# Attention with mixed heads and two MoE layers: value products leave PSUM one step later, between the reciprocals and the post-mix

## Chip, cores and metric

One NeuronCore of one Trainium2 chip runs the whole program. The metric is the device time of one execution in microseconds (us), as the median of several runs. Engines are named as in the profile: PE (TensorE matmul), PEld (TensorE weight load), DVE (VectorE), ACT (ScalarE), POOL (GpSimd), SP (SyncE, which issues DMAs).

## What is computed

Two batches, 12 heads, 448 positions, head size 64. The scores of all heads are mixed by a 12x12 matrix ahead of the softmax, and the attention weights by another one behind it. The result, 896 rows of 768, goes through two feed-forward layers. Cut from the reference:

```
scores = scale * np.matmul(q, k.transpose(0, 1, 3, 2))
scores = np.einsum('bhij,hg->bgij', scores, w_pre)
scores = scores - np.max(scores, axis=-1, keepdims=True)
attn = np.exp(scores)
attn = attn / (np.sum(attn, axis=-1, keepdims=True) + 1e-09)
attn = np.einsum('bhij,hg->bgij', attn, w_post)
x = np.matmul(attn, v)            # then laid out as 896 x 768
h = x @ w_in;  g = h * np.clip(h + 3.0, 0.0, 6.0) / 6.0;  x = g @ w_out
h = x @ w_in2; g = np.maximum(h, 0.0) + alpha * np.minimum(h, 0.0); out = g @ w_out2
```

## The kernel before

The query rows are cut into 8 tiles of 120, 120, 120 and 88 rows for each batch. Each tile is cut into groups of 10 rows (120 rows of the mixing: 10 rows times 12 heads), 90 groups in all. A main loop takes two groups (a pair) in each of its steps; step p, from 0 to 44, works on pair p. The order of the instructions on every engine is the order in which this loop is written, there is no scheduler behind it. In the middle of the loop a step issues:

- PE: the pre-mix of pair p (tile name mx, L199), then one scores product of a later tile (sc, L174), then the post-mix of pair p-1 (pt, L238), then a value product (av, L281), most often one, at some steps two, at some none.
- DVE: two maxima over mx (nm, L205), half of the copies of sc into S (L551), the reciprocals of the sums (sm, L221 and L222). ACT: two exponentials (e, L214), the other half of the copies of S, two copies of pt into MT (L253). POOL scales the post-mix weights by the reciprocals (wr, L226); in the last 8 steps DVE does it. Both also convert weights of the first feed-forward layer in some steps (wb, wst, whi, wlo).

`av(ti, a)` makes the value product of heads 2a and 2a+1 of tile ti: 16 instructions, which the trace shows as 32 passes. They go into two PSUM tiles, `av_ps[0][0]` for one half of the keys (z = 0) and `av_ps[0][1]` for the other (z = 1); the order within the product alternates between the two. Three values of a fill the pair of tiles. The pool has `bufs=2` for the tag "av", so there is just this one pair of them: when a is 0 or 3, the next three products need both tiles empty again.

A full pair is emptied ("evacuated") by one ACT copy of the first tile into xT (L291) and one DVE addition of the second tile to it (L292); 88-row tiles take two of each. Before the change both stand right behind the third product, at the end of that step.

The eight PSUM banks are all in use: two each for mx, pt, av and sc.

The places of the value products, step by step, follow from `av_at`: the third and the sixth product of a tile (a = 2 and a = 5) fall into steps 9, 12, 15, 18, 20, 22, 25, 28, 31, 34, 37, 40, 43 and 44 for tiles 0 to 6. The first product of the next three falls into the very next step at 10, 13, 16, 19, 21, 26, 32 and 38. Behind steps 22, 28, 34 and 40 there is a step without a value product first (23, 29, 35, 41). In step 43 the next product stands in the same step.

Of the kernel before, what the change touches and what calls it, by code (L numbers as in the profile page):

```python
# [7 lines left out]
F32 = mybir.dt.float32  # L8
# [5 lines left out]
ALU = mybir.AluOpType  # L14
# [21 lines left out]
def kernel(  # L36
# [15 lines left out]
    nc = tc.nc  # L52
    _, D, H, S = k.shape
# [14 lines left out]
    tiles = []  # L68
    groups = []
    for b in range(B):  # L70
        for i0 in range(0, S, GP):
            n = min(GP, S - i0)
# [8 lines left out]
    NTILE, NG = len(tiles), len(groups)  # L81
# [25 lines left out]
    with tc.manual_schedule():  # L107
        xT = xtp.tile([128, KD, NT], F32, name="xT")
# [23 lines left out]
        def load_q(ti, *at, qs=(nc.sync, nc.sync)):  # L132
            T = tiles[ti]
            n = T["n"]
            m = H // 2 * n
            t = q_st[ti] = kq.tile([128, Z + H // 2 * GP], F32, tag="qst", bufs=2, name="qst")
            nc.gpsimd.memset(t[:, :Z], 0.0)
            z = Q + m - n + upper(n)
            if z > Z + m:
                nc.gpsimd.memset(t[:, Z + m:z], 0.0)  # L140
            at = (0, *at, H // 2)
            for x, y in zip(at, at[1:]):
                for o in range(2):
                    d = slice(D * o, D * o + D)
                    a = T["i0"] * H
                    src = q[T["b"], d, a:a + H * n].rearrange("p (j o n) -> p j o n", o=2, n=n)
                    qs[o].dma_start(
                        out=t[d, Z + x * n:Z + y * n].rearrange("p (j n) -> p j n", n=n),
                        in_=src[:, x:y, o, :],
                    )  # L150
                yield
# [33 lines left out]
        def pull(g, q=nc.sync):  # L185
            ti, o, st, xn = groups[g]
            d = d_buf[g // 2 % len(d_buf)]
            src = S_t[ti][bass.ds(Z + o, xn, step=st)] if st > 1 else S_t[ti][Z + o:Z + o + xn]
            q.dma_start(d[Z:Z + xn * H, g % 2, :], src)
# [19 lines left out]
        def exp(p):  # L209
            ms, nms = mx_t.pop(p)  # L210
            sm = sm_t[p] = late.tile([128, 2], F32, tag="sm", bufs=2, name="sm")
            for o in range(2):
                e = late.tile([128, S], F32, tag="e", bufs=4, name="e")
                nc.scalar.activation(  # L214
                    out=e, in_=ms[o][:, :S], func=ACTF.Exp, bias=nms[o], accum_out=sm[:, o:o + 1]
                )
                e_t[2 * p + o] = e

        def norm(p):
            sm = sm_t.pop(p)  # L220
            nc.vector.tensor_scalar(sm, sm, 1e-9, None, ALU.add)  # L221
            nc.vector.reciprocal(sm, sm)  # L222
            for o in range(2):
                wr = wr_t[2 * p + o] = late.tile([128, WP], F32, tag="wr", bufs=4, name="wr")
                eng = nc.gpsimd if p < late_from else nc.vector
                eng.tensor_scalar(wr, wpost, sm[:, o:o + 1], 1.0, ALU.mult, ALU.mult)  # L226
# [32 lines left out]
        def by_row(dst, src, n):  # L259
            m = n // G * G  # L260
            d, s = dst[..., :m], src[..., :m]
            if len(dst.shape) == 3:
                yield (d.rearrange("p z (x o) -> p z x o", x=G), s.rearrange("p z (o x) -> p z x o", x=G))
            else:
                yield (d.rearrange("p (x o) -> p x o", x=G), s.rearrange("p (o x) -> p x o", x=G))
            if n > m:
                yield dst[..., m:n], src[..., m:n]

        av_ps = {}

        def av(ti, a):
            T = tiles[ti]
            n = T["n"]
            if a % 3 == 0:
                av_ps[0] = [psA.tile([128, 3, GP], F32, tag="av", bufs=2, name="av") for _ in range(2)]
            p = av_ps[0]
            for t in range(NJ):
                for o in range(2):
                    for z in range(2):
                        h = 2 * a + o  # L280
                        nc.tensor.matmul(  # L281
                            p[z][64 * o:64 * o + 64, a % 3, :n],
                            v_t[T["b"], h // HC][Q * z:Q * z + JH, h % HC, t, :],
                            MT[ti][Q * z:Q * z + JH, t, h, :n], start=(t == 0), stop=(t == NJ - 1),
                            skip_group_check=True,
                        )
            if a % 3 == 2:
                c0 = T["b"] * S + T["i0"]
                x = xT[:, a - 2:a + 1, c0:c0 + n]
                for (d, s0), (_, s1) in zip(by_row(x, p[0][:, :, :n], n), by_row(x, p[1][:, :, :n], n)):  # L290
                    nc.scalar.copy(d, s0)  # L291
                    nc.vector.tensor_tensor(d, s1, d, ALU.add)  # L292
                if ti >= NTILE - 2:
                    b0 = T["i0"]
                    h, l = (y[:, a - 2:a + 1, b0:b0 + n] for y in x_pairs(1))
                    nc.scalar.copy(h, x)
                    nc.vector.tensor_tensor(l, x, h.bitcast(F32), ALU.subtract)

        qk_at, av_at = {}, {}
        for i in range((NTILE - 1) * (H // 2)):  # L300
# [118 lines left out]
        def ptile():  # L419
            if "ps6" not in P:  # L420
                return P["ps2"].tile([128, 512], F32, tag="p", name="p")
            n_ps[0] += 1
            where = P["ps6"] if n_ps[0] % 8 < 6 else P["ps2"]
            return where.tile([128, 512], F32, tag="p", name="p")
# [4 lines left out]
        def x_all(c):  # L429
            return [P[f"x{c}"].tile([128, KD, S], R, tag=f"x{z}", name=f"x{z}") for z in "hl"]  # L430

        def x_pairs(c):
            if (0, c) not in x_t:
                xs = x_all(c)
                for kk in range(KD):
                    x_t[kk, c] = [x[:, kk, :] for x in xs]
                x_whole[c] = xs
            return x_whole[c]
# [16 lines left out]
        def in_part(p, i, xs, c, k0, k1):  # L455
            for kk in range(k0, k1):
                mm3(p, [w[:, kk, :] for w in w_t[i]], xs[kk, c], kk == 0, kk == KD - 1)

        def in_chain(i, xs, c):
            p = ptile()[:, :S]  # L460
            in_part(p, i, xs, c, 0, KD)
            return p
# [32 lines left out]
        def run(a):  # L495
            for _ in a:
                pass
# [33 lines left out]
        for c in range(2):  # L531
            a = GH * c
# [3 lines left out]
        for c in range(2):  # L536
            a = GH * c
# [24 lines left out]
        for i in range(NC):  # L562
            a = 2 * (14 + 8 * i)
# [35 lines left out]
        for p_ in range(-2, NP + 1):  # L599
            if p_ == -2:  # L600
                for g in range(6):
                    if g == 2:
                        list(load_q(2))
                    pull(g)
            late_pull = None
            if 0 <= p_ < NP - 3:
                g = 2 * p_ + 6
                pull(g)
                if groups[g][0] == groups[g + 1][0]:
                    pull(g + 1)  # L610
                else:
                    late_pull = g + 1
            for f in load_at.get(p_, []):
                f()
            for ti in load_q_at.get(p_, []):
                list(load_q(ti))
            if 0 <= p_ < NP:
                premix(p_)
            two = [lambda ti=ti, j=j: qk(ti, j, "mx" if p_ < 0 and j % 2 else "sc") for ti, j in qk_at.get(p_, [])]
            pend = [f() for f in (two if p_ < 0 else two[:1])]  # L620
            if 0 <= p_ < NP:
                exp(p_)
            for s_ in pend:
                s_out(s_)
            if p_ >= 0:
                for f in two[1:]:
                    s_out(f())
            if late_pull:
                pull(late_pull)
            if 0 <= p_ < NP:  # L630
                norm(p_)
            if 1 <= p_:
                post(p_ - 1)
                post_evac(p_ - 1)
            kk = 2 * (p_ - (NP - KD // 2))
            if kk == 0:
                p0 = ptile()[:, :S]
            if 0 <= kk < KD:
                in_part(p0, 0, x_t, 0, kk, kk + 2)
            if p_ == NP:  # L640
                p1 = in_chain(1, x_t, 0)
                gs[0, 0] = g_tile(0, 0)
                run(act1(p0, gs[0, 0], 0))
            for f in also.get(2 * p_, []) + also.get(2 * p_ + 1, []):
                f()
            for ti, a in av_at.get(p_, []):
                av(ti, a)
# [2 lines left out]
                f()  # L650
        for a in range(H // 2):
            av(NTILE - 1, a)
        p2 = in_chain(2, x_t, 0)
        gs[1, 0] = g_tile(1, 0)
        run(act1(p1, gs[1, 0], 1))
# [6 lines left out]
        for f in range(NC):  # L662
            p = in_chain(f, x_t, 1)
# [134 lines left out]
```

## Time and profile before

| | |
|---|---|
| median of 3 runs | 663.63 us (663.16 to 666.03) |
| the profiled execution, its own time | 661.99 us |
| its span, first to last instruction | 660.2 us |
| PE busy | 636.3 us (96%) |
| DVE, ACT, POOL busy | 408.2, 353.2, 291.3 us (62%, 53%, 44%) |
| value products (av), first to last start | 40.3 to 202.2 us |

The profile gives times in us from the start of the span. A row of the order of time reads: start, duration, engine, line, operation, tile written <- tiles read, shapes, count, and in brackets how long the engine sat idle before it and what ended this wait. Nearly the whole span is PE's; the attention part, with the steps of the loop, lies in front of 203 us, and the feed-forward layers fill the rest.

### The profile page before, as it was taken

The page shows a single profiled execution, that of the slowest core. Times are in us where ns is not written, and L with a number is a line of the kernel's source. Part 1 is how long each engine was busy: PE and PEld are TensorE (multiplying, and loading weights), DVE is VectorE, ACT ScalarE, POOL GpSimd, SP SyncE. Part 2 cuts the span into 40 slices and gives each one's busy share as a digit, 9 for nine tenths or more (in the row PEclk, how much of TensorE's full clock was granted, in tenths as well). Part 3 has the DMA queues.
Part 4 walks back from the last instruction along what each step waited for, and adds up shares of the span by engine and source line. Part 5 has one row for each costly group of instructions (what it writes and reads, how often), then busy time and mean ns, then how long its engine had stood idle before and what let it go on. Part 6 is the DMA issues. An engine that isn't in the chain of part 4 may idle for free.

```text
span 660.2 us, 17587 instructions
## 1 busy us (share of the span) xinstructions
PE 636.3 (96%) x7464; PEld 558.9 (85%) x7464; DVE 408.2 (62%) x640; ACT 353.2 (53%) x664; POOL 291.3 (44%) x236
## 2 busy tenths in 40 slices
PE   7996999998899999999999999999999999999997
PEld 2575776686688999999999999999999999999997
DVE  4664565756446678888543643389999998334501
ACT  4785787787774665666443443434444444443310
POOL 2121131312633445545675554445554556776430
PEclk9999999999899999999999999999999999999999
DMA  6776654654401233233343233212332223445202
GB/s 167 234 241 172 181 158 150 209 182 112 145 3 49 96 129 111 97 105 133 98 144 143 96 103 137 96 50 96 109 124 102 96 95 120 139 144 208 97 0 84
DMA packets 34923, 81.82 MB, mean 124 GB/s; under 512 B 11420, under 2 KB 24988, under 8 KB 34844
## 3 DMA queue, kind: packets, MB, share of 16 engines
q1 hardware_dynamic: 34268, 80.27, 37.3%
q8 instruction: 59, 0.97, 0.6%
q10 hardware_dynamic: 576, 0.41, 0.2%
q14 instruction: 20, 0.16, 0.1%
HBM read 58.65 MB, written 2.75 MB: 93 GB/s over the span
## 4 chain that ended last, share of the span: by engine, by line
PE 78%; ACT 6%; issue 5%; POOL 4%; DMA 3%; DVE 3%; SPq 0%; POOLq 0%; ACTq 0%; DVEq 0%
PE p L451 62%; PE pt L238 5%; PE mx L199 5%; PE av L281 4%; PE sc L174 3%; ACT e L214 3%; POOL wb L373 2%; POOL wlo L384 2%; ACT MT L253 1%; DMA kst<-in_k_dram 1%; DVE nm L205 1%; DVE xT L292 1%; DMA qst<-in_q_dram 1%; DMA pull<-S 1%; ACT S L551 1%
## 5 line engine op out<-in xcount | busy, mean ns | idle before, releaser
L384 POOL TENSOR_TENSOR wlo<-wb,whi 128x768 fp32r<-128x768 f32 x64 | 126.1, 1971 | 140.2 <-ACT whi L378 140.2
L373 POOL TENSOR_TENSOR wb<-wb,wst 128x768 int32<-128x768 int32 x64 | 125.6, 1963 | 74.5 <-DVE wb L366 64.9
L451 PE MATMUL p<-xh,whi 128*128 128x448 f32 x384 | 140.2, 365 | 0.0
L451 PE MATMUL p<-xl,whi 128*128 128x448 f32 x384 | 139.7, 364 | 0.0
L451 PE MATMUL p<-gl,whi 128*128 128x448 f32 x384 | 139.4, 363 | 0.0
L451 PE MATMUL p<-gh,whi 128*128 128x448 f32 x384 | 139.2, 362 | 0.0
L451 PE MATMUL p<-xh,wlo 128*128 128x448 f32 x384 | 138.5, 361 | 0.0
L451 PE MATMUL p<-gh,wlo 128*128 128x448 f32 x384 | 138.4, 360 | 0.1
L358 DVE TENSOR_SCALAR wb<-wb 128x768 f32<-128x768 f32 x64 | 52.0, 812 | 82.8 <-ACT wb L342 82.8
L342 ACT ACTIVATE wb<-wst 128x768 f32<-128x768 f32 x64 | 58.0, 907 | 70.2 <-DMA wst<-in_w_out_dram 52.2
L378 ACT CAST whi<-wb 128x768 fp32r<-128x768 f32 x64 | 53.3, 833 | 50.4 <-PE p L451 32.3
L238 PEld LDWEIGHTS pt<-wr,e 60*64 60x64 f32 (+1 forms) x2880 | 59.8, 135 | 22.1 <-issue 11.4
L214 ACT ACTIVATE e<-mx,nm 128x448 f32<-128x448 f32 x90 | 56.4, 634 | 39.8 <-DVE nm L205 39.7
L451 PEld LDWEIGHTS p<-xh,whi 128*128 128x128 f32 x384 | 72.3, 188 | 6.1
L451 PEld LDWEIGHTS p<-gh,whi 128*128 128x128 f32 x384 | 72.1, 188 | 5.7
L451 PEld LDWEIGHTS p<-gh,wlo 128*128 128x128 f32 x384 | 71.8, 187 | 5.5 <-POOL wlo L384 0.5
L451 PEld LDWEIGHTS p<-xh,wlo 128*128 128x128 f32 x384 | 72.0, 188 | 5.2
L226 POOL TENSOR_SCALAR wr<-wpost,sm 128x60 f32<-128x60 f32 x74 | 25.3, 356 | 115.4 <-DVE sm L222 112.8
L451 PEld LDWEIGHTS p<-xl,whi 128*128 128x128 f32 x384 | 72.4, 188 | 3.6
L451 PEld LDWEIGHTS p<-gl,whi 128*128 128x128 f32 x384 | 72.1, 188 | 3.7
L366 DVE SCALAR_TENSOR_TENSOR wb<-wst,wb 128x768 uint32<-128x768 uint32 x64 | 67.5, 1055 | 1.1
L238 PE MATMUL pt<-wr,e 60*64 60x60 f32 (+1 forms) x2880 | 60.7, 221 | 7.1 <-issue 6.1
(50 smaller groups left out, 792.4 us busy)
## 6 DMA issues: line engine op xcount, KB each, us to landing
wst<-in_w_out_dram SPq DMA_DIRECT2D x32, 768.0 KB
wst<-in_w_in_dram SPq DMA_DIRECT2D x27, 768.0 KB
pull<-S SPq DMA_DIRECT2D x88, 210.0 KB
wst<-in_w_in_dram SPq DMA_DIRECT2D x10, 384.0 KB
v<-in_v_dram SPq DMA_DIRECT2D x16, 168.0 KB
out_dram<-o SPq DMA_DIRECT2D x12, 224.0 KB
qst<-in_q_dram SPq DMA_DIRECT2D x8, 180.0 KB
kst<-in_k_dram SPq DMA_DIRECT2D x4, 336.0 KB
```

Of the source, the lines that this page charges most:

```text
L199: nc.tensor.matmul(ms[r][Q * c:Q * c + Q, :S], wpre[a:z], d[a:z, c, :], start=True, stop=True)
L214: nc.scalar.activation(out=e, in_=ms[o][:, :S], func=ACTF.Exp, bias=nms[o], accum_out=sm[:, o:o + 1])
L226: eng.tensor_scalar(wr, wpost, sm[:, o:o + 1], 1.0, ALU.mult, ALU.mult)
L238: nc.tensor.matmul(ts[c][Q * z:Q * z + m, u:u + GH], e[a:a + GH, j:j + m], wr[a:a + GH], start=True, stop=True,)
L281: nc.tensor.matmul(p[z][64 * o:64 * o + 64, a % 3, :n], v_t[T["b"], h // HC][Q * z:Q * z + JH, h % HC, t, :], MT[ti][Q * z:Q * z + JH, t, ...
L342: nc.scalar.activation(t, s[:, :, 1].bitcast(F32), ACTF.Abs)
L358: nc.vector.tensor_scalar(t, t, W_MAX, W_MIN, ALU.min, ALU.max)
L366: nc.vector.scalar_tensor_tensor(u, st_t[i][:, :, 1], 0xC0000000, u, ALU.bitwise_and, ALU.bitwise_or)
L373: nc.gpsimd.tensor_tensor(n, n, st_t.pop(i)[:, :, 0].bitcast(I32), ALU.add)
L378: nc.scalar.copy(hi, b_t[i])
L384: nc.gpsimd.tensor_tensor(lo, b_t.pop(i), w_t[i][0].bitcast(F32), ALU.subtract)
L451: nc.tensor.matmul(p, wt[a], xt[c], start=(first and z == 0), stop=(last and z == 2))
```

## The change

The evacuation moves into a function of its own, `av_evac`. When the third product of a group is issued, the pair of tiles is only noted in a list. The list is emptied at one of three places, whichever comes first: at the next product with a = 0 or 3 (ahead of taking the tiles again), in the next step behind `norm(p_)` (reciprocals and scaled weights) and in front of `post(p_ - 1)`, or at the end of the attention part. No instruction is added or removed.

```
+        def av_evac():
+            while full:
+                ti, a, p = full.pop()
...
+                for (d, s0), (_, s1) in zip(by_row(x, p[0][:, :, :n], n), by_row(x, p[1][:, :, :n], n)):
+                    nc.scalar.copy(d, s0)
+                    nc.vector.tensor_tensor(d, s1, d, ALU.add)
...
         def av(ti, a):
             T = tiles[ti]
             n = T["n"]
             if a % 3 == 0:
+                av_evac()
                 av_ps[0] = [psA.tile([128, 3, GP], F32, tag="av", bufs=2, name="av") for _ in range(2)]
...
             if a % 3 == 2:
-                c0 = T["b"] * S + T["i0"]
-                x = xT[:, a - 2:a + 1, c0:c0 + n]
-                for (d, s0), (_, s1) in zip(by_row(x, p[0][:, :, :n], n), by_row(x, p[1][:, :, :n], n)):
-                    nc.scalar.copy(d, s0)
-                    nc.vector.tensor_tensor(d, s1, d, ALU.add)
...
+                full.append((ti, a, p))
...
             if 0 <= p_ < NP:
                 norm(p_)
+            av_evac()
             if 1 <= p_:
                 post(p_ - 1)
                 post_evac(p_ - 1)
...
         for a in range(H // 2):
             av(NTILE - 1, a)
+        av_evac()
```

ACT around the first evacuation (it belongs to the products of steps 7 to 9), before; a pair of exponentials begins each step:

```order
L214 ACTIVATE e,sm<-mx,nm 128x448 x2
L551 COPY S<-sc 92x448
L253 COPY MT<-pt 120x48x10 x2
L291 COPY xT<-av 128x3x120
L214 ACTIVATE e,sm<-mx,nm 128x448 x2
L551 COPY S<-sc 92x448
L253 COPY MT<-pt 120x48x10 x2
```

and after:

```order
L214 ACTIVATE e,sm<-mx,nm 128x448 x2
L559 COPY S<-sc 92x448
L253 COPY MT<-pt 120x48x10 x2
L214 ACTIVATE e,sm<-mx,nm 128x448 x2
L559 COPY S<-sc 92x448
L279 COPY xT<-av 128x3x120
L253 COPY MT<-pt 120x48x10 x2
```

The copy out of av now stands behind the two exponentials and the copy of S of step 10 and ahead of that step's two copies out of pt.

DVE at the same place, before; a pair of maxima begins each step:

```order
L205 TENSOR_REDUCE nm<-mx 128x1 x2
L551 COPY S<-sc 92x448
L221 TENSOR_SCALAR sm<-sm 128x2
L222 RECIPROCAL sm<-sm 128x2
L292 TENSOR_TENSOR xT<-av,xT 128x3x120
L205 TENSOR_REDUCE nm<-mx 128x1 x2
L551 COPY S<-sc 92x448
L221 TENSOR_SCALAR sm<-sm 128x2
L222 RECIPROCAL sm<-sm 128x2
```

and after:

```order
L205 TENSOR_REDUCE nm<-mx 128x1 x2
L559 COPY S<-sc 92x448
L221 TENSOR_SCALAR sm<-sm 128x2
L222 RECIPROCAL sm<-sm 128x2
L205 TENSOR_REDUCE nm<-mx 128x1 x2
L559 COPY S<-sc 92x448
L221 TENSOR_SCALAR sm<-sm 128x2
L222 RECIPROCAL sm<-sm 128x2
L280 TENSOR_TENSOR xT<-av,xT 128x3x120
```

The addition stood ahead of the maxima of step 10 and now stands behind its reciprocals. The order on PE, POOL and SP is the same as before. On PE step 10 ends so, after the change; the last three rows are the first value product of the next three:

```order
L238 MATMUL pt<-wr,e 64x60 [waits Activation_49,Pool_49]
L238 MATMUL pt<-wr,e 64x60 [waits Activation_49]
L238 MATMUL pt<-wr,e 64x60 x12
L238 MATMUL pt<-wr,e 56x60 x2
L238 MATMUL pt<-wr,e 64x60 [waits Pool_49]
L238 MATMUL pt<-wr,e 64x60 x13
L238 MATMUL pt<-wr,e 56x60 x2
L298 MATMUL av<-MT,v_692 64x120 [waits DMAHW1_49,PE_49,Activation_49]
L298 MATMUL av<-MT,v_692 64x120 [waits DMAHW2_49,DVE_49,PE_49]
L298 MATMUL av<-MT,v_692 64x120 x14
```

The first instruction of the product waits for ACT and the second for DVE, that is for the copy and for the addition of the group before.

The same move is made at 12 places: the evacuations that ran at the start of steps 10, 13, 16, 19, 21, 23, 26, 29, 32, 35, 38 and 41. The other four (two of tile 6, two of tile 7) keep their place on every engine.

## Rows read from the trace of the kernel before

**Rows 1.** The chain that ended last, in order of time: start, duration, what.

```profile
54.50 2.70 issue
...
202.51 302.42 PE p L451 x1511
```

**Rows 2.** Timeline of steps 8 and 9, where no evacuation stands: PE, ACT, PEld.

```profile
41.16 0.54 PE L199 MATMUL mx<-pull,wpre 64*64 64x448 f32 x1
...
42.92 0.63 ACT L214 ACTIVATE e<-mx,nm 128x448 f32<-128x448 f32 x1 [0.58 <-DVE nm L205]
...
44.16 0.52 ACT L551 COPY S<-sc 92x448 f32<-92x448 f32 x1
...
44.57 1.03 ACT L253 COPY MT<-pt 120x480 f32<-120x480 f32 x2
...
47.00 0.82 PEld L281 LDWEIGHTS av<-MT,v 56*64 56x64 f32 x32
```

**Rows 3.** Timeline of step 10, at whose start the first evacuation stands.

```profile
47.88 0.93 PE L199 MATMUL mx<-pull,wpre 64*64 64x448 f32 x8
...
48.74 0.47 ACT L291 COPY xT<-av 128x360 f32<-128x360 f32 x1
...
49.24 0.53 DVE L292 TENSOR_TENSOR xT<-av,xT 128x360 f32<-128x360 f32 x1 [1.25 <-ACT xT L291]
...
50.40 0.63 ACT L214 ACTIVATE e<-mx,nm 128x448 f32<-128x448 f32 x1 [1.19 <-DVE nm L205]
...
51.30 1.02 PE L281 MATMUL av<-MT,v 56*64 56x120 f32 x32
```

**Rows 4.** Timeline of step 43: evacuation and next product in one step.

```profile
185.21 0.48 ACT L291 COPY xT<-av 128x360 f32<-128x360 f32 x1
185.72 0.53 DVE L292 TENSOR_TENSOR xT<-av,xT 128x360 f32<-128x360 f32 x1 [1.32 <-ACT xT L291]
...
186.31 0.71 PEld L281 LDWEIGHTS av<-MT,v 56*64 56x64 f32 x27 [0.38 <-DVE xT L292]
...
186.99 0.54 PE L199 MATMUL mx<-pull,wpre 64*64 64x448 f32 x1
```

**Rows 5.** Windows, steps 10, 13, 16, 19, 21, 26, 32, 38: start:end, length, PE busy.

```profile
47.88:52.13 4.25, 3.48 (x121) 2.45 (x116) 2.49 (x7) 3.06 (x10) 0.63 (x2) 1.00 0.78 205
63.51:68.06 4.55, 3.49 (x120) 2.68 (x115) 2.46 (x6) 3.36 (x10) 0.53 (x2) 1.00 0.59 180
75.10:79.16 4.06, 4.06 (x122) 2.68 (x117) 2.43 (x6) 2.87 (x9) 0.60 (x2) 1.00 0.75 198
85.84:90.49 4.65, 4.44 (x156) 3.83 (x149) 3.64 (x9) 3.46 (x11) 1.06 (x2) 1.00 0.53 153
94.02:98.61 4.59, 4.34 (x155) 3.49 (x148) 2.50 (x7) 3.40 (x10) 2.58 (x5) 1.00 0.81 222
113.90:118.06 4.16, 3.59 (x127) 2.68 (x118) 1.98 (x6) 3.09 (x9) 0.60 (x2) 1.00 0.41 145
136.87:140.31 3.44, 3.44 (x124) 2.80 (x116) 2.16 (x6) 2.25 (x7) 0.60 (x2) 1.00 0.50 186
158.90:162.32 3.42, 3.12 (x117) 2.21 (x107) 2.34 (x7) 2.23 (x8) 0.00 (x0) 1.00 0.58 138
```

**Rows 6.** Timeline, PE at the starts of steps 36 and 42.

```profile
151.26 1.58 PE L199 MATMUL mx<-pull,wpre 64*64 64x448 f32 x8 [0.96 <-ACT e L214]
...
173.26 1.58 PE L199 MATMUL mx<-pull,wpre 64*64 64x448 f32 x8 [2.00 <-ACT e L214]
```

**Rows 7.** Timeline, PE at the start of step 39.

```profile
162.32 1.59 PE L199 MATMUL mx<-pull,wpre 64*64 64x448 f32 x8 [0.30 <-ACT e L214]
```

**Rows 8.** Windows of step 11 and of part of step 42; granted clock third from the end.

```profile
52.13:58.31 6.18, 3.48 (x119) 2.47 (x115) 2.10 (x6) 3.28 (x10) 1.19 (x4) 1.00 0.85 191
...
174.90:178.40 3.50, 3.50 (x68) 3.21 (x68) 2.01 (x6) 3.50 (x9) 2.24 (x2) 0.51 0.08 28
```

More of the change, by code (lines that the diff above doesn't have):

```diff
@@ L267, in by_row, with av_evac @@
                 yield dst[..., m:n], src[..., m:n]
-        av_ps = {}
+        av_ps, full = {}, []
+        def av_evac():
+            while full:
+                ti, a, p = full.pop()
+                T = tiles[ti]
+                n = T["n"]
+                c0 = T["b"] * S + T["i0"]
+                x = xT[:, a - 2:a + 1, c0:c0 + n]
+                for (d, s0), (_, s1) in zip(by_row(x, p[0][:, :, :n], n), by_row(x, p[1][:, :, :n], n)):
+                    nc.scalar.copy(d, s0)
+                    nc.vector.tensor_tensor(d, s1, d, ALU.add)
+                if ti >= NTILE - 2:
+                    b0 = T["i0"]
+                    h, l = (y[:, a - 2:a + 1, b0:b0 + n] for y in x_pairs(1))
+                    nc.scalar.copy(h, x)
+                    nc.vector.tensor_tensor(l, x, h.bitcast(F32), ALU.subtract)
         def av(ti, a):
@@ L274, in av @@
             if a % 3 == 0:
+                av_evac()
                 av_ps[0] = [psA.tile([128, 3, GP], F32, tag="av", bufs=2, name="av") for _ in range(2)]
@@ L287, in av @@
             if a % 3 == 2:
[L288 to L297, printed above, removed]
+                full.append((ti, a, p))
         qk_at, av_at = {}, {}
@@ L631 @@
                 norm(p_)
+            av_evac()
             if 1 <= p_:
@@ L652 @@
             av(NTILE - 1, a)
+        av_evac()
         p2 = in_chain(2, x_t, 0)
```

## The prediction

> **What bounds the kernel now.** I began with the chain that ended last, in order of time. From 202.51 us on it is an unbroken run of PE work on the feed-forward layers for 302 us [rows 1], so whatever the attention part gains or loses on PE arrives whole at the end. In the attention part I then read the timeline step by step. A step without an evacuation is PE's alone: step 8 starts with its pre-mix at 41.16 [rows 2], and passes follow on each other until the next one. A step starts here wherever its first mx pass starts.
>
> A step with an evacuation at its start, such as step 10, shows what the old place costs. The copy out of av runs at 48.74, the addition at 49.24 to 49.77, and only then may DVE take the maxima of this step: ACT idles 1.19 us for them, and the first exponential starts at 50.40, that is 2.52 us behind the start of the step [rows 3], against 1.76 us in step 8 (42.92 minus 41.16) [rows 2]. So the exponentials of 12 steps are late by 0.76 us and more. Whether PE pays for it is a second question. Its next pre-mix needs the mx tile that the exponentials empty, and the rows where PE waits for them are few: 0.96 and 2.00 us in front of steps 36 and 42 [rows 6], 0.30 in front of 39 [rows 7]. In step 10 itself PE goes from the post-mix to the value product at 51.30 with no wait for av [rows 3], since its tiles have been empty since 49.77.
>
> **What the new place costs.** ACT and DVE are in-order, so the question is when they come to the moved pair. In step 8 the first exponential stands at 1.76 us, the copy of S at 3.00 and the instruction behind it at 44.57, 3.41 us after the start of the step [rows 2]. That third slot is where the copy out of av now stands. Behind the start of such a copy the addition starts after 0.50 to 0.51 us [rows 3, 4].
>
> Step 43 shows what PE does with that, since there the next product already stands in the step of the evacuation. The copy starts at 185.21, the addition at 185.72, and the weight loads of the product go on at 186.31, having waited for the addition [rows 4]: 1.10 us behind the start of the copy. The next pre-mix starts at 186.99, 0.68 us later [rows 4], because nearly the whole product was still to do.
>
> Put together: in a step whose value product is the first of the next three, PE may go past the second instruction of that product at 3.41 + 1.10 = 4.51 us, and the step is 4.51 + 0.68 = 5.19 us long. A second product in the step adds 0.82 us [rows 2]: 6.01 us. With two tiles only for av there is nothing else that PE could fill, and everything behind it on PE (the next pre-mix, the scores, the post-mix) waits too. This holds at eight places. The excess over the present lengths [rows 5]:
>
> - step 10: 5.19 - 4.25 = 0.94
> - step 13: 5.19 - 4.55 = 0.64
> - step 16: 5.19 - 4.06 = 1.13
> - step 19, two products: 6.01 - 4.65 = 1.36
> - step 21, two products: 6.01 - 4.59 = 1.42
> - step 26: 5.19 - 4.16 = 1.03
> - step 32: 5.19 - 3.44 = 1.75
> - step 38, where no scores are left and the copy of S with its 0.41 us (44.16 to 44.57) drops out: 4.78 - 3.42 = 1.36
>
> Their sum is 9.6 us. The moved instructions themselves cost nothing more; ACT's copies out of pt come half a microsecond later, but in these steps the next post-mix is later still.
>
> Part of it may be taken up. Step 11 has a hole of 2.70 us on PE in which it waits for nothing that the profile shows [rows 1]. If that is something that comes by the clock, such as late instruction packets, a wait in step 10 shrinks the hole and step 10 costs 0; if it moves with PE, step 10 costs the full 0.94. I take 0.35, nearer to nothing, since a hole is what a late arrival looks like: 0.6 less.
>
> **What the new place gives.** First, the early maxima shorten steps that follow late exponentials. The pre-mix of step 39 takes 1.59 us [rows 7] where that of step 10 takes 0.93 [rows 3]; its second half waits for the tile. Steps 27, 33 and 39 begin so. Behind the longer steps 26, 32 and 38 the exponentials will long be done. Bounds are 0 and 0.66 each; as the scores and the post-mix behind it have waits of their own, I take 0.35, or 1.0 us in all.
>
> Second, four evacuations have a step without a value product to themselves (23, 29, 35, 41), and no new wait for av. Two of these steps end with PE idle for the exponentials, 0.96 and 2.00 us [rows 6], the bound from above; from below it is nothing, as the copies out of pt, which the post-mix of the following step needs, now stand one copy of 0.47 us further back on ACT [rows 3], and in 23 and 29 that eats what the maxima gain. I take half of both, 1.5 us.
>
> Sum: 9.6 - 0.6 - 1.0 - 1.5 = +6.5 us. Against the profiled execution's own 661.99 this gives 668.5, against the median of the runs shown, 663.63, 670.1. The profiled run was below all three, so I lean to the upper one: **669.5 us**, slower by 0.9%.
>
> **The clock.** In 174.90 to 178.40 the granted clock is 0.51, between its two levels of 2.4 and 1.2 GHz mostly the lower, right behind the 2.00 us idle in front of step 42 [rows 6, 8]; at full clock that work takes half, so the dip costs about 1.75 us. Yet the window of step 11, with 2.70 us of PE idle out of 6.18, shows 1.00 [rows 8, 1]. So one idle of this size lost the clock and one did not, and the eight new waits, about 1.2 to 1.9 us each, are below both. I cost them at nothing.
> The Trainium skill speaks against that: "TensorE: Matmul & The Clock Gate", in its section on a second failure mode (PSUM queue depth cycling), says that a kernel which cycles through PSUM so that PE idles briefly between groups of matmuls, often enough, sees its clock fall and rise again and pays for it each time. By that rule the eight steps would lose the clock, and 8 x 1.75 = 14 us would come on top, some 683 us. The rows of step 11 do not bear it out.
>
> **The rivals.**
>
> - *The clock falls at the new waits.* For it: the dip in front of step 42's end and the regular spacing of the waits. Against it: step 11. Each dip costs 1.75 us; with two to four of them 673 to 677 us. Chance 0.12.
> - *Most of the wait is taken up, and nothing measurable is left.* Steps 10 and 13 for nothing (-1.0 on the sum), the whole 0.96 + 2.00 gained (-1.5), the whole 0.66 three times (-1.0), and the dip behind step 41 gone (-1.75): 6.5 - 5.2 = +1.3, or 663 to 665 us. It needs most of these together. Chance 0.15.
> - *Faster.* The value product never waits: it decides at the point where the addition of the previous three ends before PE arrives, some 2.5 us into a step in step 8's pattern instead of 4.5. Then only the gains stand, 1.0 + 1.5 and the dip of 1.75: about 660 us. It would take ACT to run the copy ahead of the exponentials, and its queue is in order. The same holds if the change left the order alone, but the order of ACT and DVE does move at 12 places. Chance 0.07.
> - *The forecast*, 0.66, with a range of its own from 665 to 674: at the low end step 10 free, both idle spans gained whole and the clock dip gone; at the high end step 10 in full, no gain behind 26, 32 and 38 (+1.0), none at 35 and 41 (+1.5), on the higher base.
>
> About 0.5%, 3.3 us, is what a measurement of this kernel tells from no change; slower starts at 666.95 us. Slower takes the clock case and nearly all of the forecast: 0.77; the same takes the second rival and the forecast's lower edge: 0.16; faster 0.07. The range that leaves out two in ten goes from 664.8 to 675.
>
> **What would show it.** In the profile after, eight steps should each have a PE wait at av for ACT's or DVE's xT, 1 to 1.9 us, some 10 us in all; before, step 43 alone has such a wait of any size. The steps should be 5.2 us long (6.0 at 19 and 21). DVE's maxima should start about 1.0 us behind the pre-mix at all 12 places, ACT's idle of 1.19 for them should be gone, and PE's 2.00 in front of step 42 should be shorter. If the waits for av are there and the time is not, they were taken up by holes like that of step 11; if they are absent, the copy did not stand where I put it; if the clock is below 1.00 near steps 10 to 38, the skill's rule was right.

## The result and the profile after

Slower: 670.76 us (median of 4 runs, 670.22 to 676.80) against 663.39 us for the kernel before on the same chip (4 runs, 661.34 to 666.03). The ratio is 1.0138, 95% interval 1.0102 to 1.0174, that is +9.2 us (+6.8 to +11.5); the two medians lie 7.4 us apart. A second measurement of the same kernel, described below as the change again, gave 1.0145 (1.0109 to 1.0182). Two of the later runs, one with the earlier k loads and one with 34 added matmuls, were in a slower state and are left out of the medians, ratios and clocks below.

The profiled execution is the slowest of the four, 676.8 us with a span of 675.0, so I read a second profile of the same kernel beside it (span 668.1). From the page of the first, the span and the clock of its slices (tenths of full speed; before, the mean over the span was 0.997, here it is 0.990):

```profile
span 675.0 us, 17585 instructions
PEclk9999798999899999999999999999999999999999
```

From the start of the last value pass to the end it is 457.96 us, before it was 457.93. So the feed-forward part is the same to 0.03 us, and but for 0.3 to 0.5 us ahead of step 0 all that is lost is lost in steps 0 to 44: 175.00 us before, 182.28 in the second profile, 189.43 in the first. The view of waits for PE, before (us in total, times, longest):

```profile
PE mx L199 <- ACT e L214: 3.7, 4, 2.0
...
PE av L281 <- ACT xT L291: 1.6, 2, 1.0
PE av L281 <- DVE xT L292: 0.6, 1, 0.6
```

and after:

```profile
PE av L298 <- ACT xT L279: 9.6, 9, 1.6
PE pt L238 <- issue: 5.6, 6, 1.4
...
PE av L298 <- issue: 3.6, 3, 2.8
PE av L298 <- DVE xT L280: 2.6, 8, 0.7
...
PE mx L199 <- ACT e L214: 0.4, 1, 0.4
```

PE's waits for the evacuation of av grew from 2.2 to 12.2 us, nine times for the copy and eight times for the addition. 9.8 of the 12.2 us lie in the eight steps foretold; the rest, in step 43 and behind step 44, was there before. Of the eight, step 32 alone has no such wait: a hole of 1.44 us in its post-mix stands in its place, and the step is 5.18 us long all the same. (A hole is idle time of PE that the profile puts down to nothing, "issue" in the view of waits.) What the change gives is there too: the waits of a pre-mix for the exponentials fell from 3.7 to 0.4 us.

The order of time in step 16, after, shows how a step looks now:

```profile
81.61 0.54 PE L199 MATMUL mx<-pull,wpre 64*64 64x448 f32 x1
...
82.63 1.16 DVE L205 TENSOR_REDUCE nm<-mx 128x1 f32<-128x448 f32 x2 [0.70 <-PE mx L199]
...
83.35 0.63 ACT L214 ACTIVATE e<-mx,nm 128x448 f32<-128x448 f32 x1 [0.54 <-DVE nm L205]
...
84.59 0.53 ACT L559 COPY S<-sc 124x448 f32<-124x448 f32 x1
...
85.00 0.48 ACT L279 COPY xT<-av 128x360 f32<-128x360 f32 x1
85.51 0.53 DVE L280 TENSOR_TENSOR xT<-av,xT 128x360 f32<-128x360 f32 x1 [0.34 <-ACT xT L279]
85.53 0.42 PE L298 MATMUL av<-MT,v 56*64 56x120 f32 x2 [0.90 <-ACT xT L279]
86.19 0.94 PE L298 MATMUL av<-MT,v 56*64 56x120 f32 x27 [0.24 <-DVE xT L280]
86.87 0.54 PE L199 MATMUL mx<-pull,wpre 64*64 64x448 f32 x1
...
177.46 0.17 DVE L222 RECIPROCAL sm<-sm 128x2 f32<-128x2 f32 x1
177.66 0.41 DVE L226 TENSOR_SCALAR wr<-wpost,sm 128x60 f32<-128x60 f32 x2
177.99 0.53 DVE L280 TENSOR_TENSOR xT<-av,xT 128x360 f32<-128x360 f32 x1
...
189.18 1.58 PE L199 MATMUL mx<-pull,wpre 64*64 64x448 f32 x8 [0.41 <-ACT e L214]
```

In step 16 the maxima start 1.02 us behind the start of the step and the exponentials 1.74, as in a step without an evacuation [rows 2]. ACT idles 0.54 us for them instead of 1.19 [rows 3]. The copy out of av is the third piece of work of ACT, at 3.39 us. The first two passes of the value product get through behind the copy, the others behind the addition, at 4.58; the next pre-mix stands at 5.26. Rows from step 38 and from the start of step 42 stand below them; they are used further down.

The eight steps whose value product needs the tiles at once, in the windows of after (length, busy time and count of PE, PEld, DVE, ACT, POOL, granted clock, DMA share, GB/s); they are steps 10, 13, 16, 19, 21, 26, 32 and 38, the lengths of before are in [rows 5]:

```profile
49.17:54.39 5.22, 4.09 (x121) 3.23 (x117) 2.82 (x8) 4.20 (x11) 1.22 (x4) 1.00 0.88 193
64.02:72.89 8.87, 4.57 (x119) 3.42 (x115) 2.56 (x6) 3.55 (x10) 0.60 (x2) 0.87 0.56 147
81.61:86.87 5.26, 4.12 (x120) 3.18 (x116) 2.91 (x8) 4.72 (x12) 1.20 (x4) 1.00 0.68 198
93.45:99.96 6.51, 4.63 (x152) 3.67 (x148) 4.68 (x11) 4.43 (x12) 1.66 (x4) 1.00 0.45 122
103.28:110.58 7.30, 5.79 (x152) 5.00 (x148) 2.88 (x8) 4.30 (x11) 3.05 (x6) 0.83 0.67 199
124.67:130.09 5.42, 3.70 (x124) 2.62 (x116) 3.61 (x11) 5.02 (x13) 1.27 (x6) 1.00 0.54 186
150.40:155.58 5.18, 3.72 (x117) 2.53 (x113) 2.55 (x6) 3.41 (x9) 0.60 (x2) 1.00 0.29 110
173.70:179.35 5.65, 3.79 (x110) 2.40 (x105) 3.00 (x11) 4.84 (x12) 0.11 (x1) 1.00 0.61 151
...
70.00:77.50 7.50, 5.66 (x97) 4.45 (x101) 2.11 (x5) 1.76 (x5) 0.00 (x0) 0.54 0.15 43
108.00:112.00 4.00, 4.00 (x72) 3.74 (x75) 0.00 (x0) 0.12 (x1) 0.00 (x0) 0.57 0.37 110
179.00:184.00 5.00, 5.00 (x135) 4.68 (x131) 1.90 (x6) 2.46 (x8) 1.83 (x1) 0.66 0.46 147
```

Five of them are 5.2 to 5.7 us long, as foretold or up to 0.2 us more, and 0.9 more in step 38. Step 13 holds a hole of 2.79 us. The last three windows are the stretches where the granted clock is low, between its two levels of 1.2 and 2.4 GHz and nearer the lower; before there was one such stretch [rows 8]. The first begins within the hole of step 13, the others behind the wait of 1.26 us in step 21 and behind the waits of step 38.

### The profile page after: what moved, and what is told of

Read it like the earlier page. It is cut to its first block, busy times and chain, and to the rows that moved or that the text cites. A ratio compares the mean times of both kernels' runs of the same rounds, so it can differ in the third digit from the quotient of the medians.

```text
span 675.0 us, 17585 instructions
## 1 busy us (share of the span) xinstructions
PE 642.2 (95%) x7464; PEld 567.1 (84%) x7464; DVE 408.4 (61%) x640; ACT 354.6 (53%) x664; POOL 289.3 (43%) x236
## 4 chain that ended last, share of the span: by engine, by line
PE 77%; ACT 7%; issue 6%; POOL 5%; DVE 3%; DMA 2%; SPq 0%; ACTq 0%; POOLq 0%; DVEq 0%
PE p L459 60%; PE av L298 5%; PE mx L199 4%; PE pt L238 4%; ACT e L214 4%; PE sc L174 3%; POOL wb L381 3%; POOL wlo L392 2%; DVE nm L205 1%; ACT MT L253 1%; DMA qst<-in_q_dram 1%; DMA pull<-S 1%; ACT S L559 1%; DVE xT L280 1%; ACT xT L279 1%
## 5 line engine op out<-in xcount | busy, mean ns | idle before, releaser
L459 PE MATMUL p<-xh,whi 128*128 128x448 f32 x384 | 138.8, 362 | 0.0
L205 DVE TENSOR_REDUCE nm<-mx 128x1 f32<-128x448 f32 x90 | 52.1, 620 | 50.3 <-PE mx L199 50.2
L238 PEld LDWEIGHTS pt<-wr,e 60*64 60x64 f32 (+1 forms) x2880 | 62.5, 137 | 21.0 <-issue 9.2
L226 POOL TENSOR_SCALAR wr<-wpost,sm 128x60 f32<-128x60 f32 x74 | 23.7, 335 | 131.6 <-DVE sm L222 129.7
L298 PE MATMUL av<-MT,v 56*64 56x120 f32 (+1 forms) x1536 | 53.7, 267 | 15.8 <-ACT xT L279 9.6
```

Source lines behind the costliest of these rows:

```text
L205: nc.vector.tensor_reduce(nm, m[:, :S], axis=AX.X, op=ALU.max, negate=True)
L238: nc.tensor.matmul(ts[c][Q * z:Q * z + m, u:u + GH], e[a:a + GH, j:j + m], wr[a:a + GH], start=True, stop=True,)
L298: nc.tensor.matmul(p[z][64 * o:64 * o + 64, a % 3, :n], v_t[T["b"], h // HC][Q * z:Q * z + JH, h % HC, t, :], MT[ti][Q * z:Q * z + JH, t, ...
L459: nc.tensor.matmul(p, wt[a], xt[c], start=(first and z == 0), stop=(last and z == 2))
```

## Experiments

Each edit is one of the changed kernel unless it says otherwise. A measured time is the median of that kernel's runs. A difference in us is what the ratio to the kernel before, run beside it on the same chip, has above 1, times the median of that (664.4, 663.7, 663.7 and 664.1 in the four groups of runs).

**Only the eight places where the tiles are needed at once.** The other four are evacuated at their step's end, as before.

```
                 full.append((ti, a, p))
+                if a == 5 and 2 <= ti <= 5:
+                    av_evac()
```

> Only the eight evacuations with a product of the next three in the very next step are deferred; the four of steps 23, 29, 35 and 41 keep the old place. Theory (PE waits for the one pair of av tiles): eight steps 5.2 us long (6.0 at 19 and 21), +9.6 - 0.6 - 1.0 = +8 us against the kernel before, so slower than the changed kernel by 1 to 2 us. Rival (the cost lies in the later copies out of pt or in something else that all twelve share): two thirds of the cost of the change, +5 us.

Measured 675.77, ratio 1.0171 (1.0135 to 1.0206), +11.4 us: more than the theory's +8, and far from the rival's +5. In its profile the eight steps take 45.9 us together, as in the second profile of the change; before they took 33.1.

**Only the four places with a step of their own** (23, 29, 35, 41), the same edit with the condition turned round:

```
+                if not (a == 5 and 2 <= ti <= 5):
+                    av_evac()
```

> Only the four evacuations behind which a step without a value product comes (23, 29, 35, 41) are deferred. Theory: no wait at av, PE's idle of 0.96 and 2.00 us in front of steps 36 and 42 shortens, -1.5 us (0 to -3) against the kernel before. Rival (cost in all twelve): +2 to +3 us.

Measured 662.35, ratio 0.9961 (0.9930 to 0.9991), -2.6 us. The two parts add up: 11.4 - 2.6 = 8.8, the change itself has 9.2 and 9.6. The waits in this kernel's profile, then the start of step 42 in the order of time and its window:

```profile
PE av L298 <- ACT xT L279: 1.6, 2, 1.0
```

```profile
176.95 1.59 PE L199 MATMUL mx<-pull,wpre 64*64 64x448 f32 x8 [0.61 <-ACT e L214]
```

```profile
176.95:185.48 8.53, 7.57 (x142) 5.68 (x146) 3.42 (x11) 5.88 (x14) 4.72 (x4) 0.80 0.30 92
```

There is no new wait for av, and of the 2.00 us idle in front of step 42 [rows 6] 0.61 are left. Yet step 42 of this profile, the slowest of twelve runs, still has a low clock, 0.80. This is the version that beats both kernels, by 0.6 to 4.7 us against the kernel before.

**The evacuation one place further back**, behind the copies out of pt:

```
-            av_evac()
             if 1 <= p_:
                 post(p_ - 1)
                 post_evac(p_ - 1)
+            av_evac()
```

> As the change, but the deferred pair stands behind the step's two copies out of pt in place of in front of them. Theory: the copy out of av comes 0.9 us later on ACT (two copies of pt take 1.03 us), each of the eight steps is 0.9 us longer, +7 us against the changed kernel, about 677 to 678. Rival (the eight steps are bound by something other than the place of the copy, such as instruction packets or the clock): about the time of the changed kernel, within 2 us.

Measured 682.47, ratio 1.0268 (1.0234 to 1.0301), +17.8, or 8.6 above the change. Step 13 (start 65.23) in the order of time, and the waits:

```profile
68.64 1.04 ACT L253 COPY MT<-pt 120x480 f32<-120x480 f32 x2
...
69.55 0.49 ACT L279 COPY xT<-av 128x360 f32<-128x360 f32 x1
...
70.09 0.42 PE L298 MATMUL av<-MT,v 56*64 56x120 f32 x2 [2.19 <-ACT xT L279]
```

```profile
PE av L298 <- ACT xT L279: 17.5, 10, 2.5
```

The copy stands at 4.32 instead of 3.41 us, and PE's wait for it grows by the same 0.9. The eight steps of this profile take 54.5 us together, 8.5 more than in the second profile of the change and so about the 8.6 by which the kernels differ. The place of one copy in ACT's order sets the time.

**Copy at the old place, only the addition later**, behind the two maxima of the next step:

```
+        adds = []
+        def add_all():
+            while adds:
+                d, s1 = adds.pop(0)
+                nc.vector.tensor_tensor(d, s1, d, ALU.add)
...    (premix, behind the two maxima)
+            add_all()
...    (av_evac, called right behind the third product)
                     nc.scalar.copy(d, s0)
-                    nc.vector.tensor_tensor(d, s1, d, ALU.add)
+                    adds.append((d, s1))
```

> The copy out of av keeps the old place on ACT; only the addition moves, behind the two maxima of the next step on DVE. Theory: the addition ends about 2.7 us into a step, PE comes to av at 2.5 us, so no wait above 0.2 us; the maxima are no longer late at 12 places; -2 to -4 us against the kernel before. Rival (the late maxima cost PE nothing): within 1 us of the kernel before. Rival (any deferral of the addition stalls av): slower than before.

Measured 663.94, ratio 0.9999 (0.9973 to 1.0024): no gain. Step 32 in its order of time, and the window of its step 12:

```profile
138.16 1.16 DVE L212 TENSOR_REDUCE nm<-mx 128x1 f32<-128x448 f32 x2 [1.38 <-PE mx L206]
...
139.24 0.52 DVE L196 TENSOR_TENSOR xT<-av,xT 128x360 f32<-128x360 f32 x1
...
139.67 1.14 PE L308 MATMUL av<-MT,v 56*64 56x120 f32 x29
```

```profile
56.54:64.11 7.57, 5.59 (x119) 4.16 (x115) 2.04 (x6) 3.68 (x9) 1.20 (x4) 0.79 0.82 200
```

The order works as meant; in step 32 the product follows with no wait, and steps 10, 26 and 32 are 3.39, 3.62 and 3.38 us long (4.25, 4.16 and 3.44 before). But step 12 has 7.57 us, with a hole of 1.98 us in the middle of its scores and a clock of 0.79 (5.20 us before). By the interval the gain is at most 1.8 us, less than the 2 to 4 of the theory; the time is that of the rival, by which late maxima cost PE nothing. That they gain and that holes eat it is argued from this one profile, not shown.

**The evacuation one place further ahead**, between the exponentials and the copies of S: `av_evac()` moved up by that much in the loop.

> As the change, but the deferred pair stands in front of the step's copies of S (behind the two exponentials on ACT, behind the two maxima on DVE). Theory (length of eight steps = place of the copy on ACT + 1.10 + 0.68 us): the copy comes 0.41 us earlier at seven places and, at step 38, the addition in front of DVE's reciprocals and scaled weights comes 0.5 us earlier; 3 to 3.5 us less than the changed kernel, +1.0% against the kernel before at most. Rival (the wait at av is set by something else): the time of the changed kernel within 1 us.

Measured 672.41, ratio 1.0128 (1.0090 to 1.0166): +8.5 us, some 1 us below the change, where 3 to 3.5 were expected; by the time alone the rival would do as well. The waits of PE, and the windows of steps 36 and 42:

```profile
PE av L298 <- ACT xT L279: 7.1, 9, 1.2
...
PE av L298 <- DVE xT L280: 1.9, 7, 0.6
PE pt L238 <- POOL wr L226: 1.8, 1, 1.8
...
PE pt L238 <- DVE wr L226: 0.8, 2, 0.6
```

```profile
158.54:166.02 7.48, 5.68 (x136) 4.48 (x140) 3.57 (x9) 4.63 (x12) 2.89 (x5) 0.77 0.32 109
182.68:190.76 8.08, 7.48 (x142) 5.45 (x146) 3.26 (x11) 5.75 (x14) 5.08 (x4) 0.79 0.27 86
```

The waits for av fell by 3.2 us as foretold (12.2 to 9.0), which is what speaks for the theory. But the addition now stands ahead of the reciprocals, and the scaled weights are late: the post-mix waits 2.6 us for them (0.7 in the change). Steps 35 and 36 together take 10.21 us (8.33), steps 41 and 42 11.16 (9.15). In both pairs the granted clock is low (0.77 and 0.79 in steps 36 and 42, 1.00 in the change), which alone is worth 1.7 us each; so the price of the late weights can't be read from them.

**Holes: the loads of the second batch's k three steps earlier**, to draw DMA traffic away from steps 11 to 13; first in the kernel before, then in the changed one, then in the one with the addition apart:

```
-            load_at.setdefault(10 + c, []).append(
+            load_at.setdefault(7 + c, []).append(
```

> The kernel before, with the four loads of the second batch's k issued in steps 7 to 10 in place of 10 to 13. If the hole of 2.70 us in step 11 and those about it come with this transfer: 2 to 4 us faster. If they are instruction packets that come late whatever is loaded, or DMA traffic that only moves: within 1 us of the kernel before.

> The changed kernel with the same earlier loads of k. If the holes of steps 10 to 13 took up a part of the waits of steps 10 and 13, the distance to the kernel before with the same loads grows against the distance measured without them, by 0.6 to 1.5 us; if they took up nothing, it stays.

> The split of the addition (copy at the old place, addition behind the next maxima) with the same earlier loads of k. If the split's gain of 2 to 4 us was given back to holes on PE that come with these loads: 3 to 5 us faster than the kernel before. If the late maxima cost nothing: the time of the kernel before with earlier loads.

Measured 667.58 (ratio 1.0049, 1.0017 to 1.0080), 669.28 (1.0107, 1.0050 to 1.0164) and 664.63 (1.0002, 0.9972 to 1.0031). None of the three gains, the kernel before loses 3.3 us. In its view of waits the holes are more, not fewer; the largest stand in steps 5, 9 and 10 now (1.27, 1.48 and 1.73 us) and that of step 11 has shrunk to 0.34:

```profile
PE pt L238 <- issue: 10.5, 12, 1.7
```

Before it was 6.1 us, 7 times. The edit did not thin the traffic as I had meant: the DMA share from 52 to 59 us is 0.89, before it was 0.84. The second and the first lie 0.6% apart with intervals that overlap, 3.9 us where it was 9.2 to 9.6 without the edit. So the distance neither grew nor stayed, which settles nothing about what the holes take up.

What the holes are, the traces show in another place. They list the DMA packets of 16 KiB that carry instructions: 59 of them before, 60, 61 and 63 in the kernels below with 144, 320 and 544 more PE passes. In the steps of all 14 profiles there are 120 holes of 0.25 us or more behind the start of step 0, and 118 of them end 1.2 to 1.8 us behind the end of such a packet, in stretches that cover 12 to 15% of the time. Counted in passes, they fall at nearly the same places in every kernel, 126 or 127 passes or a multiple of that apart: at pass 976 in 11 profiles, at 849 and 1102 in eight each. So by all that the traces show PE stands there for its next instructions; why one packet comes late and another in time is not shown.

**Work that nobody reads into the waits.** If the granted clock falls because PE idles, matmuls that fill the wait restore it. 20 matmuls of 32 columns stand behind the post-mix of the eight steps and write columns of pt which are not used otherwise:

```
                 post(p_ - 1)
+                if p_ in (10, 13, 16, 19, 21, 26, 32, 38):
+                    for i in range(20):
+                        nc.tensor.matmul(pt_t[p_ - 1][i % 2][:Q, 480:512],
+                                         wpre, wpost[:, :32], start=True, stop=True)
```

The same with 34 matmuls stands in the kernel with the evacuation further back, and with 9 in the changed one again, beside the change once more as it is.

> The changed kernel with 20 more matmuls of 32 columns in each of the eight steps, between the post-mix and the waiting value product, into columns of the pt banks that nothing reads. They lie in PE's wait (1.2 to 1.6 us) and should add little of their own. If the clock falls because of these idle spans, and that is a part of the cost: granted clock back to that of the kernel before (0.995 in the mean of its runs, against 0.993), 1 to 2 us less than the changed kernel. If the clock is not tied to them: the same clock as the changed kernel, time the same or longer by the added work.

> The variant with the pair behind the copies out of pt, with 34 such matmuls in each of the eight waits of 2.2 to 2.5 us. Without them its runs had a mean granted clock of 0.983, against 0.995 for the kernel before. If the idle spans cost the clock: back to 0.99 or more and 4 to 8 us less than the 682 us without the added matmuls. If not: clock and time unchanged.

> The changed kernel with 9 added matmuls of 32 columns in each of the eight waits in place of 20 (20 passed for 2.6 us, longer than the wait; 9 should pass in about 1.2 us and fit). The eight steps stay at 5.2 to 5.3 us (6.0 to 6.6 at 19 and 21). If the idle spans cost the clock: mean granted clock above that of the changed kernel run beside it, and 1 to 2.5 us less. If the waits alone are the cost: the same time within 1 us.

> The changed kernel itself, beside the one with 9 added matmuls on the same chip: 1.1 to 1.4% over the kernel before, mean granted clock about 0.993.

With 20: 675.54, ratio 1.0186 (1.0138 to 1.0233). The mean clock over its six runs was 0.997, in three of them 1.000. But the fill was too long, as its step 16 shows:

```profile
82.82 2.44 PE L645 MATMUL pt<-wpost,wpre 128*64 128x32 f32 x39
```

With 34: 715.97, ratio 1.0805 (1.0754 to 1.0855), and a clock of 0.974. This experiment failed: the fill takes 4.15 us at six of the eight places and 7.37 in step 10, and the copies out of pt, which stand ahead of the copy out of av on ACT, wait for it, so it tells nothing about the clock.

With 9, step 32 (start 145.09):

```profile
148.50 1.24 PE L645 MATMUL pt<-wpost,wpre 128*64 128x32 f32 x18
...
149.67 1.05 PE L298 MATMUL av<-MT,v 56*64 56x120 f32 x32
149.78 1.03 ACT L253 COPY MT<-pt 120x480 f32<-120x480 f32 x2 [0.82 <-PE pt L645]
...
150.54 0.93 PE L199 MATMUL mx<-pull,wpre 64*64 64x448 f32 x8
```

The fill fits the wait here; the step is 5.45 us long instead of 5.18. Measured 672.80, ratio 1.0133 (1.0096 to 1.0170), against 673.46 and 1.0145 (1.0109 to 1.0182) for the change beside it. The mean clock was 0.997 with the fill (1.000 in three of six runs) and 0.993 without (0.990 to 0.995). So the idle spans do lower the clock, and most of the time remains when the clock is back: PE gets to the next pre-mix when the addition is done, idle or not.

**The clock over all runs.** 161 runs of this study, without the failed fill of 34, have a time and a mean granted clock. The deviation of each from its own kernel's mean, put through one line, gives 5.2 us (plus or minus 1.0) for each 0.01 of clock. It is a fit, and a hole idles PE and can lower the clock (step 13), so the holes' own time may be in it; nor can these shares be added to those of the waits. By it the change's 0.993 against 0.995 before goes with 1.0 us, the kernel with four places (0.997) with 1.2 of its 2.6 us, the one with the evacuation further back (0.983) with 6.2 of its 17.8. The fill of 9 would get 0.0043, or 2.3 us; the difference measured, 0.8 us, has an interval of some 3.5 us to either side, so whether the added work eats a part of that is not shown. Of the eight steps in its profile step 32 is 0.27 us longer than in the change, step 10 has a hole, and the other six together are 1.8 us shorter than in the second profile.

## Why the prediction was right, point by point

**Direction and mechanism: right.** PE waits for the one pair of av tiles at seven of the eight steps foretold, for the copy of ACT and then for DVE's addition; in step 32 a hole stands in the place of the wait. Deferring only these eight costs +11.4, deferring the other four gains 2.6, and one place further back costs 8.6 more: the dose is the place of the copy in ACT's order. The rival that nothing measurable is left is out (the interval starts at 1.0102), and so is the one that the product never waits.

**The three numbers of a step: right.** Copy at 3.41, +1.10 to the second instruction of the product, +0.68 to the next pre-mix, 5.19 together; step 16 has 3.39, 1.19 (to the passes behind the addition, 86.19) and 0.68, 5.26 together. In the second profile of the changed kernel:

```profile
50.46:55.65 5.19, 3.75 (x118) 2.52 (x114) 2.55 (x6) 3.49 (x9) 0.89 (x3) 1.00 0.78 234
62.22:67.60 5.38, 3.90 (x120) 3.04 (x116) 2.87 (x8) 4.28 (x11) 1.21 (x4) 1.00 0.82 244
97.43:104.76 7.33, 5.82 (x153) 5.03 (x149) 2.88 (x8) 4.30 (x11) 3.05 (x6) 0.83 0.67 199
```

Steps 10 and 13 are 5.19 and 5.38 us long, step 13 without the hole of the other profile.

**The early maxima: right at 8 of 12 places**, about 1.0 us behind the pre-mix; they come at 1.47 in step 19, 2.40 in step 29, 1.39 in step 38 and 1.33 in step 41. PE's idle time in front of step 42 fell from 2.00 to 0.41.

**The excess of the eight steps: 9.6 foretold, 12.8 measured** in that second profile (45.93 against 33.12 us). Three terms were too small.
- Step 38, 4.78 foretold, 5.65 measured. In the last eight steps DVE scales the weights, and this stands ahead of the addition: reciprocal 177.46, two wr from 177.66, addition only at 177.99, 0.94 us behind the copy (177.05) instead of 0.50. The copy itself comes 0.35 us later than I had it, since the maxima start at 1.39.
- Step 19, 6.01 foretold, 6.51 measured. DVE has 11 instructions here and 4.68 us of work (8 and 2.88 in step 21); the maxima start at 1.47 us, not 1.0.
- Step 21, 6.01 foretold, 7.30 and 7.33 measured, both at a granted clock of 0.83. This is the clock which I had costed at nothing.

**The hole of step 11: not priced by any run.** Steps 10 to 12 took 15.64 us before, 14.84 and 11.76 in the two profiles after. So step 10's cost is gone in the holes there and more: 4.8 us come back in steps 11 and 12 of the second profile alone. In the kernel with only the eight places the same three steps take 16.63, that is the whole cost of step 10 on top. These holes differ from run to run, and no single pair of profiles prices them; the 0.6 was a guess whose sign two profiles bear out and the third does not. What I named as an example, instruction packets that come late, is what the holes are; that a hole can take up a wait is what step 32 shows.

**Shorter followers: too much.** Steps 27, 33 and 39 were to give 0.35 each. They changed by +0.40, +0.01 and -0.61 in the second profile: 0.2 in all, not 1.0.

**The four free places: the sign right, the size within the noise.** 1.5 foretold; by themselves they give 2.6 (interval 0.6 to 4.7), of which 1.2 go with the clock by the fit. The mean clock of that kernel is 0.997. The dip of 1.75 us behind the idle of 2.00 [rows 6, 8] I had left out of this term; it is gone in both profiles of the change but not in this kernel's own, where step 42 has a clock of 0.80.

**The clock: nothing foretold, about 1 us measured by the fit.** In the profiled execution three low stretches cost 7.5 x 0.46, 4.0 x 0.43 and 5.0 x 0.34, together at most 6.9 us (PE idles in a part of the first) against 1.75 before, and this run has 676.8 us, the case of the rival with two to four dips. It is not the usual run: over the 10 runs of the change the mean clock is 0.993. The Trainium skill's rule, "TensorE: Matmul & The Clock Gate", section on a second failure mode (PSUM queue depth cycling), was right that short idles which come again cost clock, and the fill shows it (0.993 to 0.997). Its price as I worked it out, 14 us for eight dips, was far too much, since even in the execution with three low stretches six of the eight steps pass at 1.00. My argument against it from step 11 alone was too narrow.

**The sum.** The misses partly cancel: +3.2 on the eight steps (the clock of step 21 is in it) and +0.8 on the followers, against -1.1 for the free places and what the holes took up beyond 0.6, which has no price of its own. +6.5 became +7.4 by the medians, +9.2 by the ratio. That the figure came out this near is in part luck: in the second profile the steps lose 7.3 us in all; the eight lose 12.8, and 4.8 come back in steps 11 and 12, where that execution has no hole and the one before had two.

**Open.** Why the kernel with the addition apart, which has the early maxima and next to no wait, gains nothing; and why some instruction packets come late. The holes are there in every kernel profiled, and which of them are long differs from profile to profile.

## What to carry to other kernels

An evacuation put off is free if the next product that needs its PSUM buffer is a step away (a second pair of tiles was not tried, the banks being full); so look at who takes the buffer next, and defer by place, not everywhere (here 4 of 12 places give 2.6 us, the other 8 cost 11.4). Price the move by the slot in which the moved instruction lands on each in-order engine, with all that stands ahead of it in that very step, since conversions and scaled weights on DVE made two of eight steps half a microsecond to a microsecond longer than foretold. Moving it one slot ahead took 3.2 us off this wait and put 1.9 on that for what it had been put in front of.

## What the hardware showed that I had not expected

- Holes on PE that the profile puts down to nothing: 2.70 us in step 11 before, 2.79 in step 13 after, 1.98 in step 12 of the kernel with the addition apart. With the k loads three steps earlier those in front of post-mixes came earlier and summed to 10.5 us in place of 6.1. Nearly all holes (118 of 120) end 1.2 to 1.8 us behind the end of an instruction packet, at places of PE's passes that recur from kernel to kernel.
- A matmul of 32 columns is 2 passes here, and the 40 passes of 20 such matmuls took some 2.5 us, 63 ns for each pass, as the rows of the fill show (39 in 2.44 us).
- A copy out of a PSUM tile waits in this program for matmuls into columns of it that it doesn't read: ACT's copies out of pt (480 columns) waited 0.82 us for the 9 matmuls into columns 480 to 511. The profile infers this wait from semaphores, so it does not show whether the chip would need it.
